# W2 and Wo of three chunks in four lanes of 32 rows around the next chunk's scores: a layer of window attention and gated MLP on one core

## The chip, the cores and the metric

The kernel runs on one NeuronCore of a Trainium2 chip. The time is the device time of one execution in microseconds. Its inputs and its output lie in the chip's memory, in bfloat16; sums are kept in float32 in PSUM, which has 8 banks of 512 columns. Names of engines: TensorE (PE; PEld is its weight load), VectorE (DVE), ScalarE (ACT), GpSimd (POOL) and SyncE (SP), which issues most of the DMAs.

## What is computed

For x of 2048 rows by 576, with 32 heads of 18 numbers, a window of 256 keys, and a hidden width of 4608:

```python
def _A_ref(x, wqkv, wo):
    B, S, D = x.shape
    H = 32; Dh = D // H; W = 256
    qkv = (lambda x, *d: x.transpose(*d))((x @ wqkv).reshape(B, S, 3, H, Dh), 2, 0, 3, 1, 4)
    q, k, v = qkv[0], qkv[1], qkv[2]
    scores = jnp.einsum("bhqd,bhkd->bhqk", q, k) * (Dh ** -0.5)
    idx = jnp.arange(S)
    mask = (idx[:, None] - idx[None, :] >= 0) & (idx[:, None] - idx[None, :] < W)
    scores = jnp.where(mask[None, None], scores, -1e9)
    p = _softmax(scores, axis=-1)
    o = jnp.einsum("bhqk,bhkd->bhqd", p, v)
    return (lambda x, *d: x.transpose(*d))(o, 0, 2, 1, 3).reshape(B, S, D) @ wo

def _B_ref(x, w1, w3, w2):
    gate = jnp.einsum("bsd,df->bsf", x, w1)
    up = jnp.einsum("bsd,df->bsf", x, w3)
    h = _silu(gate) * up
    out = jnp.einsum("bsf,fd->bsd", h, w2)
    return out

xn = _layernorm(x, axis=-1)
return x + _A_ref(xn, A_wqkv, A_wo) + _B_ref(xn, B_w1, B_w3, B_w2)
```

## The kernel before

The rows are worked off in four chunks of 512. A chunk has three parts on TensorE, one after the other.

First Q, K and V (`proj_part`): pairs of matmuls, one on rows 0 to 63 of the array and one on rows 64 to 127, with 512 columns for Q and K and 288 for V. Q and K are evacuated to `stage`, and DMAs repack them into `qv` and `kv` (`span_main`, `span_last`), four heads to a group, eight groups.

Then 36 units (`unit_pairs`), each of 128 hidden columns: nine pairs of matmuls of 512 columns for gate and up. ACT takes a tanh of the gate (`unit_tanh`), DVE forms the hidden value from it in two instructions (`unit_h`) and writes it to `hT`. Three pairs of PSUM banks rotate through the units. Between the pairs stand the steps of the scores: `scores` writes for one group, four heads at once, the scores of several blocks of 64 keys, 512 columns in two banks; `exps` is one exponential of 1024 columns on ACT; `masks` multiplies the diagonal blocks with a mask on POOL. A group has 5 steps (4 in chunk 0). When two groups are done, `pv` multiplies them with V, in tiles of 64 rows by 20 columns, eight of them side by side: the first pass after unit `FIRST`, the next two joined at `JOINT`, the last one after the units. Its result is turned, divided and packed into `oT` by DVE, POOL and DMAs.

Last W2 and Wo (`p2_item`): `hT` is the stationary operand, in blocks of 128 by 128, and W2 streams through it with 288 columns per matmul, 288 matmuls; `oT` with Wo is added to the same four banks, 32 matmuls on 128 rows and twice four on 64 rows (`wo_rest`). DVE adds x and SP stores the rows.

The order is written by the program: `add` puts each operation on the list of its engine, `resolve` derives the semaphore waits, and each engine works its list off in order. `later` puts work of DVE, POOL and SP behind a given unit; `spaced_step` spreads the score steps; `owe_part` hands out W13 loads (weights of gate and up, three buffers of four units each), `load_w2` the pieces of W2 (four buffers). Finished scores lie in slots (`pt` and buffers that are free at the time).

## Time and profile before

| | |
|---|---|
| median of 3 runs | 557.67 us (557.61 to 558.14) |
| span of the profiled execution (first to last instruction) | 555.9 us |
| one chunk's Q, K, V and units in that span (155.0 to 239.3) | 84.3 us |
| one chunk's W2 and Wo in that span (239.3 to 279.0) | 39.7 us |
| HBM read, written | 71.29 MB, 2.36 MB |
| DMA packets | 127217 |

The profile's page gives the span only, not the profiled execution's time with what lies around the span; the runs' median is 1.8 us above the span. Busy times on the page are sums per engine. Matmuls are pipelined, so a matmul's own length is longer than the distance from its start to the next one's. In the timeline a row is a group of like instructions: start, length from the first start to the last end, engine, line, operation, out<-in, shapes, count.

### The profile page before, as it was taken

The page shows a single profiled execution, that of the slowest core. Times are in us where ns is not written, and L with a number is a line of the kernel's source. Part 1 is how long each engine was busy: PE and PEld are TensorE (multiplying, and loading weights), DVE is VectorE, ACT ScalarE, POOL GpSimd, SP SyncE. Part 2 cuts the span into 40 slices and gives each one's busy share as a digit, 9 for nine tenths or more (in the row PEclk, how much of TensorE's full clock was granted, in tenths as well). Part 3 has the DMA queues.
Part 4 walks back from the last instruction along what each step waited for, and adds up shares of the span by engine and source line. Part 5 has one row for each costly group of instructions (what it writes and reads, how often), then busy time and mean ns, then how long its engine had stood idle before and what let it go on. Part 6 is the DMA issues. An engine that isn't in the chain of part 4 may idle for free.

```text
span 555.9 us, 15754 instructions
## 1 busy us (share of the span) xinstructions
PE 552.1 (99%) x6772; PEld 346.6 (62%) x6772; DVE 311.4 (56%) x583; ACT 260.0 (47%) x359; POOL 162.7 (29%) x385
## 2 busy tenths in 40 slices
PE   8999999999999999999999999999999999999998
PEld 4666554677665545477766544847776554455776
DVE  6566978610365888851056687874105577678211
ACT  6457766100387774700048787550005777756000
POOL 5424534300034452530003454333001334333000
PEclk9999999999999999999999999999999999999999
DMA  9995989577377469756826748485582674553552
GB/s 244 201 206 139 211 188 243 106 196 186 90 143 164 114 138 167 217 136 174 203 57 140 169 126 198 123 205 136 151 187 54 138 174 122 150 151 82 142 150 65
DMA packets 127217, 85.96 MB, mean 155 GB/s; under 512 B 34452, under 2 KB 124908, under 8 KB 127148
## 3 DMA queue, kind: packets, MB, share of 16 engines
q1 hardware_dynamic: 125523, 83.49, 64.1%
q10 hardware_dynamic: 1624, 1.47, 1.0%
q8 instruction: 53, 0.87, 0.7%
q14 instruction: 17, 0.13, 0.1%
HBM read 71.29 MB, written 2.36 MB: 133 GB/s over the span
## 4 chain that ended last, share of the span: by engine, by line
PE 99%; ACT 0%; DVE 0%; issue 0%
PE ps L713 50%; PE ps L785 25%; PE ps L461 10%; PE ps L587 6%; PE ps L644 3%; PE ps L792 3%; PE ps L827 1%; PE ps L699 0%; PE ps L406 0%; ACT xnT L413 0%; DVE ofin L803 0%; DVE oq L821 0%
## 5 line engine op out<-in xcount | busy, mean ns | idle before, releaser
L713 PE MATMUL ps<-xnT,w 64*128 64x512 bf16 x1400 | 185.4, 376 | 0.0
L713 PE MATMUL ps<-xnS,w 64*128 64x512 bf16 x1120 | 154.0, 376 | 0.0
L785 PE MATMUL ps<-w,hT 128*128 128x288 bf16 x1156 | 146.7, 286 | 0.0
L728 DVE SCALAR_TENSOR_TENSOR gs<-th,ps 128x512 bf16<-128x512 bf16 x144 | 97.8, 679 | 76.6 <-ACT th L722 75.8
L785 PEld LDWEIGHTS ps<-w,hT 128*128 128x128 bf16 x1156 | 112.5, 98 | 28.9 <-issue 0.4
L713 PEld LDWEIGHTS ps<-xnT,w 64*128 64x128 bf16 x1400 | 73.0, 94 | 60.0 <-DVE ofin L653 0.2
L722 ACT ACTIVATE th<-ps 128x512 bf16<-128x512 f32 x144 | 85.6, 594 | 44.4 <-PE ps L713 42.0
L731 DVE SCALAR_TENSOR_TENSOR hT<-gs,ps 128x512 bf16<-128x512 bf16 x144 | 98.9, 687 | 4.9
L713 PEld LDWEIGHTS ps<-xnS,w 64*128 64x128 bf16 x1120 | 58.1, 94 | 46.7
L596 ACT ACTIVATE pt<-ps 128x1024 bf16<-128x1024 f32 (+1 forms) x70 | 70.8, 1011 | 31.2 <-PE ps L587 30.9
L474 ACT ACTIVATE stage<-ps 128x512 bf16<-128x512 f32 x16 | 9.5, 596 | 142.0 <-PE ps L461 142.0
L803 DVE TENSOR_TENSOR ofin<-ps,xp 128x288 bf16<-128x288 f32 x31 | 13.4, 455 | 108.3 <-PE ps L699 58.1
L623 POOL TENSOR_TENSOR hT<-hT,mk 128x128 int32<-128x128 int32 (+1 forms) x59 | 24.0, 429 | 170.5 <-ACT hT L596 170.3
L623 POOL TENSOR_TENSOR pt<-pt,mk 128x128 int32<-128x128 int32 (+1 forms) x124 | 49.9, 427 | 28.8 <-ACT pt L596 28.8
L587 PE MATMUL ps<-qv,kv 64*128 64x320 bf16 (+4 forms) x528 | 52.8, 260 | 0.0
L587 PEld LDWEIGHTS ps<-qv,kv 64*128 64x128 bf16 x528 | 27.4, 94 | 26.2 <-ACT hT L596 1.5
L596 ACT ACTIVATE w<-ps 128x1024 bf16<-128x1024 f32 (+1 forms) x32 | 32.3, 1010 | 12.3 <-PE ps L587 12.2
L461 PE MATMUL ps<-xnT,wp 64*128 64x512 bf16 (+1 forms) x360 | 38.0, 355 | 0.0
L596 ACT ACTIVATE hT<-ps 128x1024 bf16<-128x1024 f32 (+1 forms) x32 | 32.3, 1010 | 5.3 <-PE ps L587 4.8
L623 POOL TENSOR_TENSOR w<-w,mk 128x128 int32<-128x128 int32 (+1 forms) x56 | 22.9, 429 | 28.8 <-ACT w L596 28.8
L666 DVE STREAM_TRANSPOSE od<-oq 128x256 bf16<-128x256 bf16 x64 | 25.8, 427 | 6.9 <-POOL oq L659 6.9
L461 PEld LDWEIGHTS ps<-xnT,wp 64*128 64x128 bf16 x360 | 19.0, 94 | 14.4 <-ACT stage L474 0.2
(93 smaller groups left out, 384.9 us busy)
## 6 DMA issues: line engine op xcount, KB each, us to landing
w<-in_B_w_dram SPq DMA_DIRECT2D x210, 192.0 KB, 3.9
w<-in_B_w_dram SPq DMA_DIRECT2D x72, 288.0 KB, 3.3
xp<-in_A_x_dram SPq DMA_DIRECT2D x30, 144.0 KB, 4.5
out_dram<-ofin SPq DMA_DIRECT2D x31, 72.0 KB, 1.7
xnS<-xnT SPq DMA_DIRECT2D x8, 256.0 KB, 4.2
oT<-od SPq DMA_DIRECT2D x40, 36.0 KB
pt<-in_A_wqkv_dram SPq DMA_DIRECT2D x4, 288.0 KB, 6.0
hT<-in_B_w_dram SPq DMA_DIRECT2D x6, 192.0 KB, 5.2
```

Of the source, the lines that this page charges most:

```text
L461: op = add("pe", lambda e, out_=out_, st=st, mv=mv, n=n, r0=r0, first=first: e.matmul(out_, st, mv, start=first, stop=(part == 1 and n == ...
L587: add("pe", lambda e, r0=r0, out_=out_, kb=kb, q0=q0, nb=nb: e.matmul(out_, kb4[r0:r0 + 64, g, kb + NV - NB, :] if kb < 0 else kv[r0:r0 + ...
L596: add("act", lambda e: e.activation(pt_slot(sl)[:, 0:w, :], PS[:, SC[0]:SC[1] + 1, 0:w].rearrange("p r q -> p q r"), ACT.Exp, scale=scale) ...
L623: add("pool", lambda e, vb=vb, mm=mm: e.tensor_tensor(vb, vb, mm, ALU.mult), r=(key if n == 0 else []) + ["mk"], **{"w" if n == 0 else "j" ...
L644: add("pe", lambda e, p=p, q=q, pr=pr, sl=sl, g=g, pos=pos, q0=q0, nb=nb, col=col, first=first, n=n: e.matmul(PS[32 * q:32 * q + VW, banks ...
L666: add("dve", lambda e: e.transpose(od[i][:, g % 2, c0:c0 + CH // 2], oq[:, c0:c0 + CH // 2]), r=["oq", "oq0"], **{"j" if half or g % 2 els ...
L713: op = add("pe", lambda e, n=n, r0=r0, r=r, k=k, src=src: e.matmul(PS[:, b0 + r, :], wt[r0:r0 + 64, k, fl * 128:(fl + 1) * 128], src, star ...
L722: add("act", lambda e: e.activation(th[i][:], PS[:, bg, :], ACT.Tanh, scale=0.5), r=[("ps", bg)], w=[("th", i)])
L728: add("dve", lambda e: e.scalar_tensor_tensor(out=gs[i][:], in0=th[i][:], scalar=1.0, in1=PS[:, bg, :], op0=ALU.add, op1=ALU.mult), r=[("t ...
L731: add("dve", lambda e: e.scalar_tensor_tensor(out=hT[:, u, :], in0=gs[i][:], scalar=0.5, in1=PS[:, bu, :], op0=ALU.mult, op1=ALU.mult), r= ...
L785: add("pe", lambda e: e.matmul(bank, hT[:, f, tt * 128:(tt + 1) * 128], w2[sl][:, k, n0:n1], start=first, stop=(c + 1 == NC and half == 1 ...
L792: add("pe", lambda e: e.matmul(bank, oT[:, k, tt * 128:(tt + 1) * 128], wo[:, k, d0 + n0:d0 + n1], start=False, stop=(k == 3 and (half == ...
```

## The change

For the W2 part of chunks 0, 1 and 2, the array is used as four lanes of 32 rows and 128 columns (`w2_lanes`). W2 is now stationary and `hT` streams, 512 columns per matmul: lane a holds rows 32a to 32a+31 of every 128 hidden columns and sums into its own bank; for each of four blocks of 128 output columns it has 36 matmuls of W2 and 4 or 5 of Wo. At the end of a block `finish` adds the four banks (two copies on ACT, three additions on DVE), and a DMA turns the result. Four banks are summed into while the four others take scores. The last 64 output columns follow as 41 pairs of matmuls of 256 columns, side by side in two tiles of 64 output columns.

Q, K and V of the next chunk move ahead of this part, from behind it. Sixteen of the next chunk's heads (groups 0 to 3) get their scores in the lanes, between the matmuls of W2: one head per lane, 18 rows, blocks of 128 keys, three steps of 512 columns per head (`score_new`), an exponential of 512 columns (`exps_new`), and a mask that DVE applies (`masks_new`). Their P V (`pv_new`) runs on all 128 rows in tiles of 20 columns, four side by side, in two passes: one after two groups, within the lanes, the other after the last 64 columns of W2. Groups 4 to 7 stay between the units in the old form, and their two P V are joined (`JOINTS`). The chunk's result is added to x and stored in units 4 to 7 of the next chunk. Chunk 3 has its W2 and Wo as before. W2 is loaded in pieces of 9 blocks by 128 columns (and 18 by 64), W13 in two halves per block from its third block on, where six parts were.

```diff
@@ load_w2 @@
+        def w2_by(s, nd):
+            return w2[s][:, :, :].rearrange("p f d -> p (f d)").rearrange("p (f d) -> p f d", d=nd)
+
...
+            if n2fill <= (NC - 1) * 2 * NFC:
+                if m < 16:
+                    dst, f0, nf, d0, nd = w2_by(s, 128), m % 4 * 9, 9, m // 4 * 128, 128
+                else:
+                    dst, f0, nf, d0, nd = w2_by(s, 64), (m - 16) * 18, 18, 512, 64
+                add("sp", lambda e: e.dma_start(
+                    dst, B_w2[f0 * 128:(f0 + nf) * 128, d0:d0 + nd].rearrange("(fl p) d -> p fl d", p=128)),
+                    w=[("w2", s)], after=after, dma=f"w2_{s}")
+                return
...
+        STEPS = [[(-2, 0, 1), (0, 0, 3)], [(-1, 0, 2), (2, 2, 2)], [(1, 1, 3), (3, 3, 1)]]
+        EDGES = [[(0, 2, 0), (3, 1, 0)], [(1, 2, 0)], [(2, 2, 0), (0, 1, 1)]]
...
+        def score_new(g, s, a, b, n):
+            jb, q0, nb = STEPS[s][n]
+            c0 = 128 * n * STEPS[s][0][2]
+            add("pe", lambda e: e.matmul(
+                PS[:, b, c0:c0 + nb * 128], kn[32 * a:32 * a + Dh, g, W + 128 * jb:W + 128 * jb + 128],
+                qv[32 * a:32 * a + Dh, g, q0 * 128:(q0 + nb) * 128], start=True, stop=True, tile_position=(32 * a, 0)),
+                r=[("knp" if jb < 0 else "kn", g), ("q", g)], **{"j" if n else "w": [("ps", b)]})
+
+        def exps_new(g, s, a, b, sl):
+            p = a % 2
+            add("act", lambda e: e.activation(head_of(sl, p), PS[:, b, :], ACT.Exp, scale=scale),
+                r=[("ps", b)], **{"j" if p else "w": pt_keys(sl)})
+
...
+                mm = mkn[:, k0:k0 + nb, :].unsqueeze(1).to_broadcast([128, 2, nb, 64])
+                add("dve", lambda e, b0=b0, nb=nb, mm=mm: e.tensor_tensor(
+                    v[:, :, b0:b0 + nb, :], v[:, :, b0:b0 + nb, :], mm, ALU.bitwise_and),
+                    r=(key if n == 0 else []) + ["mkn"], **{"w" if n == 0 else "j": key})
...
+                    for p in range(2):
+                        for q in range(4):
+                            g, pr = 2 * j + q // 2, q % 2
...
+                            add("pe", lambda e, p=p, q=q, pr=pr, sl=sl, g=g, blk=blk, q0=q0, nb=nb, col=col, first=first, n=n: e.matmul(
+                                PS[32 * q:32 * q + VW, banks[p], q0 * 128:(q0 + nb) * 128],
+                                van[:, blk, 4 * g + 2 * pr + p, :],
+                                head_of(sl, p)[:, col * 128:(col + nb) * 128],
+                                start=first, stop=(n == n_all), tile_position=(0, 32 * q), skip_group_check=True),
+                                r=pt_keys(sl) + [("vn", blk)], **{"w" if new else "j": [("ps", banks[p])]})
...
+        def w2_lanes(c, live, pool_):
+            n = c + 1
+            for a in range(4):
+                for d_ in range(4):
+                    own = [("w2", d_, f) for f in range(NF)] + [("wo", d_, t) for t in range(4)]
+                    if (a < 2) == (d_ % 2 == 0):
+                        own.append(("wo", d_, 4))
+                    items[a] += [it + (k == 0, k == len(own) - 1) for k, it in enumerate(own)]
...
+            def finish(d_):
+                ls = sets[d_ % 2]
+                add("act", lambda e: e.activation(psum2, PS[:, ls[0], :], ACT.Copy), r=[("ps", ls[0])], w=[("th", 0), ("th", 1)])
+                add("act", lambda e: e.activation(psum3, PS[:, ls[2], :], ACT.Copy), r=[("ps", ls[2])], w=["psum3"])
+                for k in (1, 3):
+                    add("dve", lambda e, k=k: e.tensor_tensor(psum2, PS[:, ls[k], :], psum2, ALU.add),
+                        r=[("ps", ls[k])], w=[("th", 0), ("th", 1)])
+                add("dve", lambda e: e.tensor_tensor(gs[i][:], psum3, psum2, ALU.add),
+                    r=["psum3", ("th", 0), ("th", 1)], w=[("gs", i)])
+                events.setdefault(rounds + SEND_AFTER, []).append(("turn", d_))
...
+                if done < len(steps) and steps[done][2] * 2 + steps[done][3] == a and now >= nxt and (slots or steps[done][3]):
+                    cand = [b for b in sets[1 - d_ % 2] if b not in held]
+                    b = min(cand, key=lambda x: ready[x])
+                    if ready[b] <= now and left_in(items, at, a, clk) > 1.25:
...
+                        score_new(g, s, a, b, 0)
...
+                    add("pe", lambda e, b=b, rows=rows, wt=wt, fl=fl, k=k, a=a, first=first: e.matmul(
+                        PS[:, b, :], wt[rows, fl, :], hT[rows, k, :], start=first, stop=False, tile_position=(32 * a, 0)),
+                        r=[("h", k), ("w2", sl)], **{"w" if first else "j": [("ps", b)]})
...
+                    add("pe", lambda e, b=b, rows=rows, k=k, a=a, d_=d_, last=last: e.matmul(
+                        PS[:, b, :], wo[rows, k, d_ * 128:(d_ + 1) * 128], oT[rows, k, :], start=False, stop=last, tile_position=(32 * a, 0)),
...
+                if not pv_done and 0 in ended and not any(tail) and min(at) > 2 * 41 + 5 and now > ended[0] + PV_WAIT:
...
+                    pv_new(n, 0, cand)
...
+                        add("pe", lambda e, k=k, r=r, sl=sl: e.matmul(
+                            PS[64 * r:64 * r + 64, b, 0:256], w2_by(sl, 64)[:, k % 18, :], hT[:, k, 256 * r:256 * r + 256],
+                            start=(k == 0), stop=False, tile_position=(0, 64 * r), skip_group_check=True),
...
+                        add("pe", lambda e, t=t, r=r, wt=wt: e.matmul(
+                            PS[64 * r:64 * r + 64, b, 0:256], wt, oT[:, t, 256 * r:256 * r + 256],
+                            start=False, stop=(t == 4), tile_position=(0, 64 * r), skip_group_check=True),
...
+            banks = job()
+            pv_new(n, 1, banks)
+            add("dve", lambda e: e.tensor_copy(orem, PS[:, b, 0:256]), r=[("ps", b)], w=["orem"])
+            add("sp", lambda e: e.dma_start_transpose(frem, orem), r=["orem"], w=["frem"], dma="tr4")
...
+        def fin_add(tt):
+            x = xp[fin_xs[tt]]
+            r, j = divmod(tt, 2)
+            add("dve", lambda e: e.tensor_tensor(fin[:, tt, 0:512], fin[:, tt, 0:512], x[:, 0:512], ALU.add),
+                r=[("xp", fin_xs[tt])], w=[("fin", tt)])
...
-        FIRST = {0: 14, 1: 11, 2: 8, 3: 11}
-        JOINT = {0: (27, 6), 1: (27, 5), 2: (24, 8), 3: (27, 8)}
-        AHEAD = [40, 24, 40, 24]
+        FIRST = 15
+        JOINTS = [(27, 6), (31, 6), (32, 5), (25, 7)]
+        AHEAD, ALL_DONE = 40, [0, 276, 284, 215]
+        W2_FIRST, W2_SPACE, PV_WAIT = 2.2, 0.53, 3.0
+        W2_REPACK, SEND_AFTER = 40, 15
+        W2_EVENTS = {148: (("part",),), 156: (("part",),)}
...
-                        spaced_step()
+                fin_xs[:] = load_four(c - 1)
+                pv_out(late_pv[0], 0)
+                pv_out(late_pv[1], 1)
+                o_scale(0)
...
+            if c + 1 < NC:
+                if c == 0:
+                    banks = job()
...
+                for m, what in enumerate(PROJ_LATER + [None]):
+                    got = proj_begin(c + 1, what) if what else proj_end()
+                    if m == 0:
...
+                    if got == ("q", 2):
+                        new_k(0)
+                        new_k(1)
...
+                    if 3 <= m < 7:
+                        new_q(m - 3, "act")
+                    owe_part(last_pe())
+                i_last = (job_ctr - 1) % 3
+                live = [*SC, *JOBS[(i_last + 1) % 3]]
+                late_pv = w2_lanes(c, live, [*JOBS[(i_last - 1) % 3], *JOBS[i_last]])
+                continue```

How this moves the instructions. On PE, before, from the last P V of chunk 0 into W2 (`w2_0` to `w2_3` are the four buffers of W2; L644 is P V, L785 W2, L792 Wo):

```order
L644 MATMUL ps<-pt,va 20x320 x8
L644 MATMUL ps<-pt,va 20x128 x8
L785 MATMUL ps<-w2_0,hT 128x288 x16
L785 MATMUL ps<-w2_1,hT 128x288 x16
L785 MATMUL ps<-w2_2,hT 128x288 x16
L785 MATMUL ps<-w2_3,hT 128x288 x16
```

And in the changed kernel, from the end of the next chunk's Q, K, V (L496) into the lanes (L1036 is W2 in lanes, L756 a part of a score step):

```order
L496 MATMUL ps<-xnT,wp 128x256 x8
L496 MATMUL ps<-wv,xnT 128x288 x8
L1036 MATMUL ps<-hT,w2_0 128x512 x36
L1036 MATMUL ps<-hT,w2_1 128x512 x8
L756 MATMUL ps<-qv,kn 128x128
L1036 MATMUL ps<-hT,w2_1 128x512 x3
L756 MATMUL ps<-qv,kn 128x384
L1036 MATMUL ps<-hT,w2_1 128x512 x4
L756 MATMUL ps<-qv,kn 128x128
L1036 MATMUL ps<-hT,w2_1 128x512 x3
L756 MATMUL ps<-qv,kn 128x384
L1036 MATMUL ps<-hT,w2_1 128x512 x8
```

A score step is a matmul of 128 and one of 384 columns (or 256 and 256) in the same lane; two steps come to 18 matmuls of W2, and a W2 buffer now serves 36 of them.

On PE, before, at the end of W2 of chunk 0 and into the next chunk's Q, K, V (L461; L699 is the rest of Wo on 64 rows):

```order
L785 MATMUL ps<-w2_1,hT 128x288 x4
L792 MATMUL ps<-wo,oT 128x288 x4
L699 MATMUL ps<-wo,oT 128x288 x4
L461 MATMUL ps<-xnT,wp 128x512 x28
L461 MATMUL ps<-wv,xnT 128x288 x10
```

And in the changed kernel (L1045 is Wo in lanes, L1086 and L1096 the last 64 columns, and L791 the first of the 48 matmuls of the new P V, behind which the next chunk's units begin):

```order
L1036 MATMUL ps<-hT,w2_3 128x512 x36
L1045 MATMUL ps<-oT,wo 128x512 x18
L1086 MATMUL ps<-hT,w2_0 64x256 x36
L1086 MATMUL ps<-hT,w2_1 64x256 x36
L1096 MATMUL ps<-oT,wo 64x256 x8
L1096 MATMUL ps<-oT,wz 64x256 x2
L791 MATMUL ps<-stage,va 20x128 x2
L791 MATMUL ps<-pt,va 20x128 x2
```

W2 now ends in the tail of 64 columns and a P V, and the Q, K, V that stood here are gone.

On ACT, which had no instruction during W2 of chunk 0, the changed kernel has this in the lanes (L763 are exponentials of scores, L987 and L988 the copies of `finish`):

```order
L547 ACTIVATE va<-ps 64x8x18 x2
L763 ACTIVATE pt<-ps 128x512 x11
L987 ACTIVATE thb<-ps 128x512
L988 ACTIVATE kv<-ps 128x512
L763 ACTIVATE pt<-ps 128x512 x9
L763 ACTIVATE xp<-ps 128x512 x4
L763 ACTIVATE stage<-ps 128x512
L987 ACTIVATE thb<-ps 128x512
L988 ACTIVATE kv<-ps 128x512
```

The copies that empty the lanes' banks stand behind the exponentials of the scores before them.

496 lines of the change are left out of this document (374 added, 122 removed).

## Prediction

> **What bounds the kernel now.** I read the page first, then the chain, then the timeline of TensorE stage by stage.
>
> ```profile
> span 555.9 us, 15754 instructions
> PE 552.1 (99%) x6772; PEld 346.6 (62%) x6772; DVE 311.4 (56%) x583; ACT 260.0 (47%) x359; POOL 162.7 (29%) x385
> PE ps L713 50%; PE ps L785 25%; PE ps L461 10%; PE ps L587 6%; PE ps L644 3%; PE ps L792 3%; PE ps L827 1%; PE ps L699 0%; PE ps L406 0%; ACT xnT L413 0%; DVE ofin L803 0%; DVE oq L821 0%
> ```
>
> TensorE is the whole chain, and nothing else has a visible share of it: gate and up L713, W2 L785, Q K V L461, scores L587, P V L644, Wo L792. A busy PE need not be PE at its peak, so I measure the pace by starts in the timeline of chunk 1 (start us, us, what):
>
> ```profile
> 92.44 8.63 PE ps L713 x80
> ...
> 237.68 0.41 PE L699 MATMUL ps<-wo,oT 64*128 64x288 bf16 x4
> 238.03 0.32 PE L644 MATMUL ps<-stage,va 64*20 64x320 bf16 x4
> ...
> 239.34 16.34 PE L785 MATMUL ps<-w,hT 128*128 128x288 bf16 x132
> 255.52 0.65 PE L792 MATMUL ps<-wo,oT 128*128 128x288 bf16 x4
> ...
> 278.06 0.65 PE L792 MATMUL ps<-wo,oT 128*128 128x288 bf16 x4
> 278.64 0.42 PE L699 MATMUL ps<-wo,oT 64*128 64x288 bf16 x4
> 278.90 1.46 PE L461 MATMUL ps<-xnT,wp 64*128 64x512 bf16 x12
> ```
>
> The first row is from the chain: 40 pairs of 64-row matmuls in 8.63 us, 0.216 us a pair of 512 columns. A W2 matmul of 288 columns takes (255.52 - 239.34)/132 = 0.1226 us. The two paces give 0.417 ns a column and some 0.0025 us per instruction, and the stretches join without holes: the kernel is a list of columns on one engine. So the change pays only through fewer columns, less cost per instruction, or fewer changes between tile shapes; any wait it brings is paid in full.
>
> **The change, part by part (chunks 1 to 3 for scores and P V, 0 to 2 for W2).**
>
> Scores. The rows of one score step between units:
>
> ```profile
> 174.88 0.32 PE L587 MATMUL ps<-qv,kv 64*128 64x320 bf16 x2
> 175.02 0.27 PE L587 MATMUL ps<-qv,kb 64*128 64x128 bf16 x4
> 175.10 1.26 PE L713 MATMUL ps<-xnT,w 64*128 64x512 bf16 x10
> ```
>
> A step takes 175.10 - 174.88 = 0.22 us; a chunk has 8 groups of 4 heads with 5 steps, 8.8 us. Afterwards four groups keep this form, 20 x 0.22 = 4.4 us. The other 16 heads take 3 steps each, 48 steps that each stream 512 columns through one of four lanes: 48 x 0.216/4 = 2.6 us. That is 8.8 - 7.0 = 1.8 us a chunk, **-5.4 us** in three. It is the main gain: four lanes write 512 scores per column where two write 256, and a block of 128 keys needs 384 queries instead of 320 for 64.
>
> W2 and Wo. Before: 0.35 us for the four L699 ahead of P V, and 278.90 - 239.34 = 39.56 us, together 39.9 us. After: a lane holds 4 x (36 + 4) matmuls and 2 of the rest of Wo, 162 rounds. The trace has no four lanes, so I bound a round: 0.216 us is what two lanes of 512 columns take, and no row streams 512 columns faster; if only two of the four ran at once it would be 0.432. I take 0.216, because the nearest rows on concurrency are the L644 matmuls above, eight tiles that share one stream: 96 of them between 238.03 and 239.34. So 162 x 0.216 = 35.0 us. The last 64 columns of W2 are 41 pairs of 256 columns; the nearest rows are the pairs of 256 of L461:
>
> ```profile
> 291.57 0.62 PE L461 MATMUL ps<-xnT,wp 64*128 64x256 bf16 x8
> 292.01 0.67 PE L461 MATMUL ps<-wv,xnT 64*128 64x288 bf16 x8
> ```
>
> 0.44/4 = 0.11 us a pair, 4.5 us. Sum 39.5 us, -0.4 us a chunk, **-1.2 us**.
>
> P V. One pass alone takes 239.34 - 238.03 = 1.31 us. Two joined:
>
> ```profile
> 217.05 1.37 PE L644 MATMUL ps<-pt,va 64*20 64x320 bf16 x96
> ...
> 219.50 0.82 PE L713 MATMUL ps<-xnS,w 64*128 64x512 bf16 x6
> ```
>
> 2.45 us, so a second one costs 1.14 and a trip into this shape and out again 0.17. A chunk had 2.45 + 2 x 1.31 = 5.07 us. The new form streams 12 blocks x 128 x 2 = 3072 columns per tile where the old one has 2560: 1.14 x 3072/2560 = 1.37, with the trip 1.54 (bounds 1.37 and 1.54). Chunk after: 2.45 + 2 x 1.54 = 5.53, +0.46, **+1.4 us** in three.
>
> Changes of shape. The four L792 from 278.06 take 4 x 0.1226 = 0.49 us at pace, but L699 starts after 0.58: 0.09 us a change. Q K V to lanes and lanes to the last 64 columns are two more per chunk (bounds 0 and 0.17 each), **+0.5 us**. Q, K and V have the same matmuls, only earlier; chunk 3's W2 stays as it was.
>
> Sum: -5.4 - 1.2 + 1.4 + 0.5 = **-4.7 us**.
>
> **What must stay hidden.** Q, K, V ahead fill the 13 us between the last unit and W2, and W2 in lanes now hides 48 exponentials and 8 copies that were not there. In that stretch before:
>
> ```profile
> 239.30:279.00 39.70, 39.70 (x334) 31.54 (x328) 6.60 (x17) 0.00 (x0) 4.69 (x11) 1.00 0.69 174
> L722 ACT ACTIVATE th<-ps 128x512 bf16<-128x512 f32 x144 | 85.6, 594 | 44.4 <-PE ps L713 42.0 <-DVE hT L731 1.5
> 60.61 0.60 ACT L722 ACTIVATE th<-ps 128x512 bf16<-128x512 f32 x1 [0.38 <-PE ps L713]
> 61.10 0.91 ACT L596 ACTIVATE pt<-ps 128x896 bf16<-128x896 f32 x1
> L731 DVE SCALAR_TENSOR_TENSOR hT<-gs,ps 128x512 bf16<-128x512 bf16 x144 | 98.9, 687 | 4.9
> ```
>
> (columns: PE, PEld, DVE, ACT, POOL busy, clock, DMA share, GB/s). ACT had 0.00 us there, DVE 6.60, and the granted clock was 1.00. A 512-wide ACT instruction lasts 0.594 us, but the next can start 0.49 us after it (60.61 to 61.10). In the order of the lanes two score steps come per 18 W2 matmuls: 4.5 rounds x 0.216 + 2 x 0.054 = 1.08 us, one exponential per 0.54 us. That lies between the two ends, nearer to the pace of 0.49, which I take: 56 x 0.49 = 27.4 us in some 39. Scores use the four PSUM banks of the next 128 columns, each again after four steps, 2.2 us. DVE gets 40 masks, no wider than half an L731, and 12 additions as wide, at most 40 x 0.4 + 12 x 0.69 = 24 us (the 0.4 is my estimate from half of 0.687), and the masks are needed only by P V, 3 us and more later.
>
> The result of a chunk is now added and stored in units 4 to 7 of the next one, on DVE, which has room in that stage:
>
> ```profile
> 155.00:239.30 84.30, 84.30 (x1231) 45.38 (x1226) 63.78 (x116) 59.24 (x77) 34.85 (x83) 1.00 0.72 158
> ```
>
> 63.78 of 84.30 us. The 64-key masks of half the heads leave POOL there, and half the exponentials leave ACT. If DVE fell behind, units would wait for PSUM, but eight additions of at most 0.69 us spread over four units can't make up the 20 us that are free.
>
> The queues. W2 pieces of 288 KB now have 256 B to a packet instead of 576:
>
> ```profile
> q1 hardware_dynamic: 125523, 83.49, 64.1%
> w<-in_B_w_dram SPq DMA_DIRECT2D x72, 288.0 KB, 3.3
> ```
>
> A packet holds an engine 0.641 x 16 x 555.9/125523 = 45 ns for 665 B on average. A piece was 32 packets per engine, 1.5 of its 3.3 us; it becomes 72, between 72 x 45 x 256/665 = 1.3 us (by bytes) and 3.3 us (by count), so it lands 3.1 to 5.1 us after its issue. It is issued when its buffer's old piece is used up and needed three pieces later, 27 rounds = 5.8 us: hidden at both ends. SP's other work that moves into the lanes (repacking of groups 4 to 7, five transposes, two W13 halves) waits for engines that are ahead; a late transpose would hold W2 loads queued behind it. The four Q moves are on ACT's queue between evacuations of Q K V, where no exponential waits any more. The W13 weights of four units still come two such blocks ahead, 8 x 9 x 0.216 = 15.6 us, now in two halves instead of six parts.
>
> The Trainium skill (DMA: Bandwidth & Descriptors, Specifications) asks for at least 512 B to a transfer and says that below this there is a read-modify-write. It speaks against 256 B pieces: at half the rate per byte a piece would take 3.0 us instead of 1.5 and land after about 4.8, an estimate, which is still inside the lead. The mixed packets above cannot decide it.
>
> **Rivals.**
>
> *A, the lanes do not overlap: slower.* Each further lane starts behind the one before it. Two 320-column matmuls cover 0.32 us (row at 174.88), and one lasts 0.297:
>
> ```profile
> L587 PE MATMUL ps<-qv,kv 64*128 64x320 bf16 x256 | 39.8, 297 | 0.0
> ```
>
> so a lane starts 0.02 us after the other. If two more lanes lengthen each round by that, it is 0.26 us, 486 rounds x 0.044 = +21 us, **574 us**; with two at a time, +105 us. It decides from 4.7/486 = 10 ns a round on. Against it: eight tiles of L644 share a stream without this. For it: those write 20 columns each, and no row has more than two tiles of 128. The Trainium skill (TensorE: Matmul & The Clock Gate, Part 3, measured speedup) gives 3.07x for four row tiles of 32 instead of 4; as a lasting pace that would be an estimate of 0.216 x 4/3.07 = 0.281 us a round, +32 us, 585 us. No run here shows it.
>
> *B, ACT falls behind.* If an exponential costs 0.594 us and not 0.49, a burst of 14 ends 14 x 0.054 = 0.76 us late, the copies that empty the banks come behind it, and TensorE waits 0.3 to 0.7 us at each of 12 block changes: +3.6 to +8.4 us, **556.6 to 561.4**, no change or slightly slower. For it: the exponential waits for TensorE each time. Against: 0.49 in the rows.
>
> *C, a moved transfer is late* (a W2 piece behind a transpose on SP, or Q and K of the new heads at the first score): 0.5 to 1 us at some 10 places, **558 to 563**.
>
> **How the numbers follow.** The page's span is 555.9 us; the runs' median, 557.67, lies 1.8 us above it, which I take as the part around the span, unchanged. Forecast 557.7 - 4.7 = **553.0 us**. Its own range: without the trips and changes of shape 551.5, and 0.0025 us less per round if instructions cost nothing in the lanes, 550; with a few small waits 555.5. Chances: forecast 0.72, A 0.11, B 0.11, C 0.06. A change below 0.2% (1.1 us) can't be told from none. Range 550 to 558.5: it leaves out A, most of C and the far half of B. Faster (under 556.5): 0.72 and a third of B and C, 0.78. Same: 0.06. Slower: 0.16.
>
> **What would show it.** Lanes: 36 matmuls of W2 ahead of the first score in 9 x 0.216 = 1.9 us and the stage in about 39 us (A: over 45). PE without idle time in the lanes, ACT some 30 us busy there (B: PE idle behind ACT copies at the block changes). A score step in units still 0.22 us, 20 per chunk. W2 pieces landing under 5.8 us (C). I am wrong if a round of four is over 0.226 us, or if TensorE stops for PSUM banks.

## Result: 554.2 us where 557.7 was, and the profile after

The changed kernel took a median of **554.22 us** (552.73 to 556.97, six runs) beside 557.75 us (557.61 to 558.14, six runs) for the kernel before: a ratio of 0.9939, 95% interval 0.9921 to 0.9956. The same kernel once more (e1) took 553.51 us (553.23 to 554.77, five runs) beside 557.69, ratio 0.9927, interval 0.9913 to 0.9940. So it is 0.6 to 0.7% faster, 3.5 and 4.2 us. The forecast was 553.0 us in a range of 550.0 to 558.5. The profiled run took 553.22 us with a span of 551.5.

From the page of the changed kernel, the lines that answer to those of before: the span, the engines, the chain, and two DMA queues (packets, MB, share).

```profile
span 551.5 us, 17660 instructions
PE 547.4 (99%) x7690; PEld 302.4 (55%) x7690; DVE 364.5 (66%) x745; ACT 294.5 (53%) x481; POOL 120.5 (22%) x281
PE ps L860 51%; PE ps L1036 17%; PE ps L496 10%; PE ps L932 6%; PE ps L682 4%; PE ps L1086 2%; PE ps L1045 2%; PE ps L739 2%; PE ps L791 2%; PE ps L756 1%; DMA wv<-in_A_wqkv_dram 1%; PE ps L939 1%; PE ps L1096 0%; SPq L311 0%; ACT xnT L447 0%; PE ps L846 0%
q1 hardware_dynamic: 164622, 85.42, 79.1%
q8 instruction: 60, 0.98, 0.8%
```

The chain is still TensorE, now with the lanes (L1036, L1045, L756) in it, and it has a new first link: 1% of it is the load of V's weights. ACT and DVE do 35 and 53 us more than before, POOL 42 us less. DMA engines are busy for 79% in place of 64%. By the DMA records, packets of 128 to 576 bytes make a quarter of this rise (W2 comes in 256 bytes now, the last two pieces of a chunk in 128). Two thirds are in packets of 1024 bytes, nearly all W13's: about as many as before, but 84 ns each in place of 67. The queue of instruction fetches, 60 packets of 16 KB, was no part of the prediction; it comes up below.

The three stretches of lanes, by windows of the changed kernel (busy us and count of PE, PEld, DVE, ACT and POOL; granted clock, DMA share, GB/s); a stretch lasts 39.3 us with the new P V in it, of which the windows leave out the last 1.4:

```profile
115.90:153.80 37.90, 37.90 (x774) 21.10 (x776) 22.66 (x60) 30.14 (x57) 1.35 (x2) 1.00 0.71 139
251.30:289.20 37.90, 37.90 (x774) 21.26 (x776) 22.62 (x60) 30.14 (x57) 1.35 (x2) 1.00 0.70 137
386.80:424.70 37.90, 37.90 (x774) 21.39 (x776) 22.67 (x60) 30.14 (x57) 1.35 (x2) 1.00 0.75 147
```

All three are alike: no hole on PE, clock 1.00, ACT busy for 30.14 of 37.90 us, DVE for 22.7. The timeline of PE at the start and the end of the first stretch:

```profile
115.86 2.55 PE L1036 MATMUL ps<-hT,w 32*128 32x512 bf16 x44
118.24 0.22 PE L756 MATMUL ps<-qv,kn 18*128 18x128 bf16 x1
...
155.12 4.12 PE L1086 MATMUL ps<-hT,w 128*64 128x256 bf16 x72
...
159.72 0.23 PE L791 MATMUL ps<-stage,va 128*20 128x128 bf16 x2
...
161.14 1.04 PE L860 MATMUL ps<-xnT,w 64*128 64x512 bf16 x8
```

The first score comes after 44 matmuls, as in the order shown under the change; the prediction had counted 36 and 1.9 us. They take 118.24 - 115.86 = 2.38 us, 0.0541 each or **0.216 us a round of four**. The new P V takes 161.14 - 159.72 = 1.42 us. In the same stretch, grouped by line and shape (busy us and mean ns; then the idle time ahead and its releaser):

```profile
L763 ACT ACTIVATE pt<-ps 128x512 bf16<-128x512 f32 x40 | 21.7, 594 | 2.6 <-PE ps L756 2.5
L771 DVE TENSOR_TENSOR pt<-pt,kv 128x256 int32<-128x256 int32 x20 | 8.3, 422 | 8.3 <-ACT pt L763 8.1
```

ACT waits for TensorE's scores (2.5 us), not the other way round. From the start of each group of TensorE to the start of the next, summed by kind of work over the whole execution (us, worked out from the starts in the two traces):

```
                                   before    after
units (L713, L860)                 280.38   280.43
scores between units (L587, L682)   33.37    19.74
W2 and Wo, 128 rows (L785, L932 ..) 159.96    40.19
lanes, their scores included            -   113.54
last 64 columns (L1086, L1096)          -    13.79
P V, old form (L644, L739)          19.09    11.29
P V, new form (L791)                    -     8.53
Q, K, V (L461, L496)                52.86    53.83
before and between these             6.59     6.56
sum                                552.25   547.90
```

### The profile page after: what moved, and what is told of

Read it like the earlier page. It is cut to its first block, busy times and chain, and to the rows that moved or that the text cites. A ratio compares the mean times of both kernels' runs of the same rounds, so it can differ in the third digit from the quotient of the medians.

```text
span 551.5 us, 17660 instructions
## 1 busy us (share of the span) xinstructions
PE 547.4 (99%) x7690; PEld 302.4 (55%) x7690; DVE 364.5 (66%) x745; ACT 294.5 (53%) x481; POOL 120.5 (22%) x281
## 3 DMA queue, kind: packets, MB, share of 16 engines
q1 hardware_dynamic: 164622, 85.42, 79.1%
## 4 chain that ended last, share of the span: by engine, by line
PE 98%; DMA 1%; SPq 0%; ACT 0%; issue 0%; DVE 0%
PE ps L860 51%; PE ps L1036 17%; PE ps L496 10%; PE ps L932 6%; PE ps L682 4%; PE ps L1086 2%; PE ps L1045 2%; PE ps L739 2%; PE ps L791 2%; PE ps L756 1%; DMA wv<-in_A_wqkv_dram 1%; PE ps L939 1%; PE ps L1096 0%; SPq L311 0%; ACT xnT L447 0%; PE ps L846 0%
## 5 line engine op out<-in xcount | busy, mean ns | idle before, releaser
L860 PE MATMUL ps<-xnT,w 64*128 64x512 bf16 x1400 | 177.0, 376 | 0.0
L860 PE MATMUL ps<-xnS,w 64*128 64x512 bf16 x1120 | 147.8, 376 | 0.0
L875 DVE SCALAR_TENSOR_TENSOR gs<-thb,ps 128x512 bf16<-128x512 bf16 x144 | 97.8, 679 | 60.6 <-ACT thb L869 60.0
L869 ACT ACTIVATE thb<-ps 128x512 bf16<-128x512 f32 x144 | 85.6, 595 | 77.1 <-PE ps L860 76.2
L1036 PE MATMUL ps<-hT,w 32*128 32x512 bf16 x1728 | 106.9, 374 | 0.0
L860 PEld LDWEIGHTS ps<-xnT,w 64*128 64x128 bf16 x1400 | 67.2, 94 | 70.2
L860 PEld LDWEIGHTS ps<-xnS,w 64*128 64x128 bf16 x1120 | 53.9, 94 | 58.1
L1036 PEld LDWEIGHTS ps<-hT,w 32*128 32x128 bf16 x1728 | 57.6, 92 | 29.6 <-issue 1.4
L763 ACT ACTIVATE pt<-ps 128x512 bf16<-128x512 f32 x120 | 65.1, 594 | 7.7 <-PE ps L756 7.5
L756 PE MATMUL ps<-qv,kn 18*128 18x384 bf16 (+2 forms) x288 | 54.5, 267 | 0.0
L771 DVE TENSOR_TENSOR pt<-pt,kv 128x256 int32<-128x256 int32 x96 | 31.3, 371 | 24.5 <-ACT pt L763 24.1
L496 PE MATMUL ps<-xnT,wp 64*128 64x512 bf16 (+1 forms) x360 | 38.2, 355 | 0.1
L932 PE MATMUL ps<-w,hT 128*128 128x288 bf16 (+1 forms) x292 | 36.9, 284 | 0.0
L756 PEld LDWEIGHTS ps<-qv,kn 18*128 18x128 bf16 x288 | 26.5, 93 | 14.4 <-DVE uq L800 0.8
L932 PEld LDWEIGHTS ps<-w,hT 128*128 128x128 bf16 x292 | 28.2, 98 | 7.4 <-issue 0.5
L682 PE MATMUL ps<-qv,kv 64*128 64x320 bf16 (+4 forms) x336 | 31.7, 258 | 0.0
```

What stands on the lines that cost most here:

```text
L496: op = add("pe", lambda e, out_=out_, st=st, mv=mv, n=n, r0=r0, first=first: e.matmul(out_, st, mv, start=first, stop=(part == 1 and n == ...
L682: add("pe", lambda e, r0=r0, out_=out_, kb=kb, q0=q0, nb=nb: e.matmul(out_, kb4[r0:r0 + 64, g - GN, kb + NV - NB, :] if kb < 0 else kv[r0: ...
L756: add("pe", lambda e: e.matmul(PS[:, b, c0:c0 + nb * 128], kn[32 * a:32 * a + Dh, g, W + 128 * jb:W + 128 * jb + 128], qv[32 * a:32 * a + ...
L763: add("act", lambda e: e.activation(head_of(sl, p), PS[:, b, :], ACT.Exp, scale=scale), r=[("ps", b)], **{"j" if p else "w": pt_keys(sl)})
L860: op = add("pe", lambda e, n=n, r0=r0, r=r, k=k, src=src: e.matmul(PS[:, b0 + r, :], wt[r0:r0 + 64, k, fl * 128:(fl + 1) * 128], src, star ...
L869: add("act", lambda e: e.activation(th[i][:], PS[:, bg, :], ACT.Tanh, scale=0.5), r=[("ps", bg)], w=[("th", i)])
```

## The experiments

Each starts from the changed kernel. "Lanes" is the time from the first lane matmul to the last 64 columns, without the P V among them, a chunk: 37.85 us in the changed kernel. Where an edit adds lines, the numbers behind it shift: L1038 and L1039 are L1036 of the changed kernel, L1088 is L1086, L861 and L863 are L860.

### e1: once more

No edit.

> The changed kernel once more, nothing edited, to see whether its runs scatter again and where. Seen so far: 552.7 to 557.0 us (median 554.22), the kernel before 557.6 to 558.1. Theory (the list of columns on TensorE is as forecast, and what scatters is a wait for a weight transfer, at the start or at the lanes): the stages of the new trace agree with the first one within 0.1 us each, apart from the first 22 us or the start of the lanes; median 552.7 to 554.5. Rival (ACT or DVE falls behind in the lanes in some runs, B): the lanes L1036+L756+L1045 take more than 38.2 us a chunk in a slow profile, where the first trace has 37.85.

553.51 us, lanes 37.85 us again, units 280.43. What differed from the first trace was Q, K, V at the start (0.2 us) and the joined P V of chunk 0, 2.30 us in place of 1.92. Its weight loads, in the timeline of e1:

```profile
83.15 0.08 PEld L739 LDWEIGHTS ps<-w,va 64*20 64x20 bf16 x1 [0.30 <-issue]
```

TensorE stopped in the middle of a P V with nothing to wait for that the profile shows. So ACT does not make this scatter, and waits for weights make no more than the 0.2 us at the start; what "issue" stands for had to be found.

### e2 and e3: the price of a score in the lanes

```diff
+            for k in range(2):      # e2: each score matmul twice
                 add("pe", lambda e: e.matmul(PS[:, b, c0:c0 + nb * 128], kn...
```
```diff
-                PS[:, b, c0:c0 + nb * 128], kn...          # e3: an eighth of the columns
+                PS[:, b, c0:c0 + nb * 16], kn...
-            ... e.activation(head_of(sl, p), PS[:, b, :], ACT.Exp, scale=scale)
+            ... e.activation(head_of(sl, p), PS[:, b, :], ACT.Copy)
```

> Every score matmul of the 16 heads in the lanes is issued twice in a row into the same PSUM columns. Theory (a step costs its 512 columns in one of four lanes, 0.054 us, and nothing waits): 144 x 0.054 = +7.8 us against the changed kernel, the lanes 40.4 us a chunk. A second matmul in the same lane right behind the first waits for it, so if neighbours in the queue must be of different lanes to overlap, it costs up to 0.216 us more than its share: 144 x 0.16 = +23 us. Rival B (the stage is set by ACT): less than +4 us, since TensorE would only fill time in which it waits.

> Every score matmul in the lanes streams an eighth of its columns, and the 48 exponentials of a chunk are copies of the same shape (the scores of these 16 heads are not computed, ACT has the same work). Theory (columns): 7/8 of 7.8 us goes, -6.8 us against the changed kernel, lanes 35.6 us a chunk. If a score matmul costs a fixed time beside its columns (its weights, its place in the queue): -3 to -5 us. Rival B (ACT sets the pace): within 1.5 us of the changed kernel.

e2: 564.84 us (564.15 to 567.87), lanes 40.78 us, so 2.93 us a chunk or 0.061 us a step. That is the priced 0.054 and a little, and not the 0.216 that a second matmul of the same lane would add if it held the others up. e3: 547.94 us (547.81 to 548.28), 5.6 us less than e1; lanes 36.07 us, 1.78 us less. Seven eighths of the columns were priced at 2.26 us a chunk; about 0.5 us, 10 ns a step, stays with the step and not with its columns. Rival B (ACT sets the pace) is out here: TensorE's time followed its own work both ways.

Of e2's profiled span, 14.6 us longer, only 8.8 are lanes. 3.2 us are in old P V and 2.4 in units. The timeline of PE in e2, in the middle of the joined P V of chunk 2 and behind it, and the windows around it (columns as above, the clock third from the end):

```profile
375.47 0.23 PE L739 MATMUL ps<-pt,va 64*20 64x128 bf16 x2 [1.87 <-issue]
...
376.56 2.06 PE L861 MATMUL ps<-xnT,w 64*128 64x512 bf16 x10
```
```profile
376.50:380.50 4.00, 4.00 (x26) 1.49 (x22) 3.03 (x7) 0.60 (x1) 0.58 (x1) 0.57 0.02 4
380.50:384.20 3.70, 3.70 (x38) 1.66 (x36) 2.71 (x5) 1.20 (x2) 0.10 (x1) 1.00 0.58 128
```

A stop of 1.87 us, again put down to issue, and behind it four microseconds at a granted clock of 0.57, in which ten matmuls took 2.06 us (1.26 in the row at 175.10 of before). This stop is paid nearly twice; one of 2.03 us in e10, below, is not.

### e4, e8 and e11: how the lanes share the queue

```diff
+                if stick is not None:
+                    a = stick
...
                 at[a] += 1
+                stick = a if at[a] % N else None     # N = 2 (e4), 9 (e8), 4 (e11); e8 and e11 up to item 150 of a lane
```

> In the lanes each lane now issues two W2 or Wo matmuls in a row before the next lane's turn (0 0 1 1 2 2 3 3 in place of 0 1 2 3), with the same work in all. Rival A as a question of order: if TensorE starts its instructions in the order of the queue and a lane must end one matmul before its next, eight matmuls take 4 x 0.216 us instead of 2 x 0.216, so 486 rounds take 0.432 us: about +100 us (650 us). If a later instruction of a free lane may overtake, or two of one lane overlap otherwise: within 5 us of the changed kernel.

> Each lane now issues up to nine W2 or Wo matmuls in a row before the next lane's turn (e4: two in a row, no loss), with the score steps planned 0.45 us apart in place of 0.53. Theory (a lane's matmuls wait in a queue of their own while those of another lane, later in the order, start; the depth is unknown): if the look ahead is deep enough for 27 matmuls, within 2 us of the changed kernel; if it is a few matmuls, the lanes follow one another for most of nine: up to 486 x 0.216 x 0.8 = +80 us (635 us).

> Each lane issues four W2 or Wo matmuls in a row before the next lane's turn (two: no loss, 554.0 us; nine: 906.6 us), with the score steps planned 0.50 us apart. Theory (TensorE starts a matmul while a bounded number of earlier ones in other lanes still wait): if the bound is 12 or more, within 2 us of the changed kernel; if it is 4 to 8, lanes follow one another for part of each round of sixteen: a pace between 0.216 and 0.8 us a round, +20 to +250 us, and a granted clock well under 1 in the lanes as with nine.

One run each: two in a row 554.0 us (lanes 38.2 us a chunk), four 593.04 (50.6), nine 906.6 (154.2). The first 5 us of lanes in the changed kernel, by windows, and then in e4, e11 and e8, with a later stretch of e8 (PE's count is the first in brackets):

```profile
116.00:121.00 5.00, 5.00 (x102) 2.67 (x98) 1.53 (x6) 3.15 (x8) 0.00 (x0) 1.00 0.21 47
```
```profile
116.00:121.00 5.00, 5.00 (x106) 3.79 (x97) 1.23 (x5) 2.87 (x8) 0.00 (x0) 1.00 0.25 54
```
```profile
116.00:121.00 5.00, 5.00 (x78) 2.82 (x75) 1.60 (x4) 2.25 (x6) 0.00 (x0) 1.00 0.19 44
```
```profile
116.00:121.00 5.00, 5.00 (x42) 2.29 (x39) 1.19 (x3) 0.86 (x3) 0.00 (x0) 1.00 0.19 43
160.00:195.00 35.00, 35.00 (x145) 13.66 (x143) 2.90 (x9) 7.16 (x12) 0.00 (x0) 0.50 0.17 34
```

In 5 us 102, 106, 78 and 42 matmuls are under way, all at clock 1.00. With two of one lane in a row next to nothing is lost (0.3 us a chunk), so a lane that is busy does not hold up the next lane's matmul; with four a quarter is lost, and with nine the lanes mostly follow one another. In e8 it gets worse: from 126 us on the clock is 0.50, although PE counts as busy throughout, and in the stretch shown 145 matmuls take 35 us, 0.241 us each against 0.054. They have 65,536 columns, 128 times 512; at half the clock 512 columns take 0.43 us, so on average 1.6 lanes are at work. The look-ahead between lanes is real and short. How many instructions it holds was not measured; e8 and e11 also have their scores 0.45 and 0.50 us apart instead of 0.53. The values of the result also change in e8 and e11; why stays open, so that more than the order may differ there.

### e6: more work for ACT

```diff
                     exps_new(g, s, a, b, sl)
+                    if p and pr:
+                        exps_new(g, s, a, b, sl, True)
```

> In the lanes 12 of the 48 exponentials of a chunk are done twice, into the same place, so ACT has 12 x 0.594 = 7.1 us more to do in a stage of 37.85 us of which it was busy for 30.1. Theory by the sum of the stage (it still fits, and the scores' PSUM banks are four deep): within 1 us of the changed kernel. Theory by the pace (rival B just over its edge): five exponentials take 5 x 0.49 = 2.45 us where four steps come in 4 x 0.53 = 2.12, twelve times over, so ACT ends a good 4 us behind, of which the gaps between bursts and the free banks take some 1 to 2: TensorE waits 2 to 3 us a chunk, +6 to +9 us, and the waits stand at score matmuls for ACT's exponentials.

563.77 us (562.87 to 564.59), 10.3 us over e1; lanes 40.95 us, +3.1 a chunk, 9.3 in three. From what PE waited for in e6 (us in all, times, longest), and its timeline there:

```profile
PE ps L1038 <- ACT stage L763: 3.6, 3, 1.2
```
```profile
138.94 0.40 PE L1038 MATMUL ps<-hT,w 32*128 32x512 bf16 x3 [1.20 <-ACT stage L763]
```

TensorE stops at a change of 128 columns for a PSUM bank whose exponential is not done: the place that rival B names. Such stops of PE are 3.6 of the 9.3 us; the rest is waits of its weight loads and shorter gaps. 7.1 us more on ACT would still fit into the 7.8 us that it has free in a stretch; it does not fit the pace of the bursts. So the margin is under 12 exponentials a chunk.

### e7: W2 pieces asked for later

```diff
-                        if piece[m] == 4:
+                        if piece[m] == 4 and m:
                             load_w2((c + 1) * 2 * NFC)
+                        if piece[m] == 4 and m == 15:
+                            load_w2((c + 1) * 2 * NFC)
```

> In the lanes each W2 piece is asked for one piece later (nine rounds, about 2 us, less lead: when its buffer's old piece and the one after it are used up), so the lead falls from 27 rounds (5.8 us, some 6.5 with the scores between) to 18 (3.9 to 4.4 us). Rival C's margin: pieces landed a median 3.9 us after their issue, some later. Theory (the transfer was hidden by about 2 us): about half of the 12 pieces of a chunk are now late by up to 1 us, +1 to +4 us a chunk, +3 to +12 us. If the true lead is larger than I count, since TensorE's weights are read late or SP issues early: within 0.5 us of the changed kernel.

566.57 us (565.81 to 571.18), +13.1 us. But the lanes took 38.2 us: the loss is in the last 64 columns, 24.2 us in place of 11.9 for L1086, over the three chunks. What PE waited for in e7:

```profile
PE ps L1088 <- DMA w<-in_B_w_dram: 8.5, 4, 2.9
PE ps L1036 <- DMA w<-in_B_w_dram: 0.2, 1, 0.2
```

The 16 pieces of 128 columns still come in time with 2 us less lead, but for some 1 us in chunk 2, half of it a wait for the first of the last two. The last piece does not. The timeline of PE in e7 where it is needed in chunk 0, and SP's at the end of the lanes of chunk 1, first in the changed kernel and then in e7, where this stretch begins 3.9 us later (L379 issues W2 pieces, L343 W13):

```profile
159.29 3.29 PE L1088 MATMUL ps<-hT,w 128*64 128x256 bf16 x36 [2.33 <-DMA w<-in_B_w_dram]
```
```profile
287.44 0.58 SPq L379 DMA_DIRECT2D w<-in_B_w_dram  x1
288.07 1.99 SPq L343 DMA_DIRECT2D w<-in_B_w_dram  x2
```
```profile
290.29 0.59 SPq L379 DMA_DIRECT2D w<-in_B_w_dram  x1
290.92 1.33 SPq L343 DMA_DIRECT2D w<-in_B_w_dram  x1
292.30 0.62 SPq L379 DMA_DIRECT2D w<-in_B_w_dram  x1
```

Measured from the start of the stretch, the last piece is asked for only 1.0 us later (0.7 and 2.1 in chunks 0 and 2), but a W13 load of 576 KB now goes out ahead of it. It landed 7.2 and 7.4 us after its issue in chunks 0 and 2 (chunk 1 has no record), against 4.0 to 4.2 in the changed kernel. That the W13 load causes this is likely and was not tested alone. TensorE waits 2.3 to 2.9 us for it in each chunk, and the clock is 0.50 for 3.4 us behind each wait. My count of leads was right for the lanes and missed where the tight place is: the last piece. In the changed kernel that one, issued at 287.44, landed 4.0 us later and was needed at about 292.6 (18 pairs, 2.0 us, after 290.57): a margin of 1 us.

### e5 and e9: the joined P V elsewhere

```diff
-        JOINTS = [(27, 6), (31, 6), (32, 5), (25, 7)]
+        JOINTS = [(27, 6), (34, 6), (35, 5), (25, 7)]      # e5 and e9
-                if joint[0] < u:
+                if (27, 31, 32, 25)[c] < u:                # e9 only
```

> The joined P V of chunks 1 and 2 move later by 27 pairs of unit matmuls (JOINTS 31,6 to 34,6 and 32,5 to 35,5); all work is the same. Counted in TensorE's own instructions (a weight load and a matmul each, and its waits), they began at 250 and 252 of a block of 256 and ended without a stop (2.46 and 2.47 us); they now begin near 102 and 104. In e2 a joined P V that began at 124 stopped for 2.0 us in its middle with nothing to wait for but its next instructions, and the units after it ran 1.8 us longer. Theory (a stop for the next block of instructions, which a P V uses up faster than it is fetched, is what the joint's place avoids, and such stops make the scatter of the runs): +2 to +4 us for each of the two, +4 to +8 us in all, and a profile that shows P V at 4 us or more with an idle time put down to issue. Rival (the stop in e2 was a chance collision with other DMA traffic, and the place within a block does not matter): within 0.5 us of the changed kernel.

> As e5 (the joined P V of chunks 1 and 2 begin 27 pairs of unit matmuls later, near 102 and 104 of a block of 256 instructions), but W2 pieces for the lanes are asked for in the same units as in the changed kernel; in e5 they had moved behind the joint, and the lanes of chunk 2 waited 25.6 us for them. Theory (instruction blocks): each of the two stops in its middle for 2 to 4.5 us with nothing to wait for but its instructions (e5: 6.93 and 5.21 us in place of 2.46), and what follows runs up to 2.5 us longer at a lower granted clock, so +6 to +14 us against the changed kernel, with lanes of 37.9 us a chunk. Rival (e5's stops came from the moved loads): P V at 2.5 us and within 1 us of the changed kernel.

e5: 602.21 us (601.74 to 603.84). Two joined P V took 6.93 and 5.21 us, but most of the 49 us is the side effect that the second text names: W2 for the lanes of chunk 2 was asked for behind the joint. What PE waited for in e5:

```profile
PE ps L1036 <- DMA w<-in_B_w_dram: 25.6, 8, 4.2
PE ps L739 <- issue: 7.0, 3, 4.1
```

e9: 567.12 us (565.77 to 567.94), lanes 37.85 us again, the two P V 6.78 and 9.52 us. Here W2 pieces land in buffers that hold probabilities the later P V still reads, so P V waits for them and its values change. In e9's list of waits, and the timeline of PE in the first P V:

```profile
PE ps L739 <- DMA w<-in_B_w_dram: 6.7, 2, 4.8
PE ps L739 <- issue: 2.0, 1, 2.0
```
```profile
239.87 0.20 PE L739 MATMUL ps<-od,va 64*20 64x64 bf16 x3 [2.04 <-issue]
...
240.67 2.26 PE L860 MATMUL ps<-xnT,w 64*128 64x512 bf16 x10
```

So 6.7 of e9's 13.6 us are waits for these loads, and the instruction stop of 2.04 us stands at the same matmul of P V as in e5 (behind 173 weight loads), with the slow units after it. In chunk 2, where P V had already waited 4.8 us, it has no stop at that point: probably the wait gave the fetch its time. So the theory's range of +6 to +14 us is met only with waits that were not in its sum, and of its two stops one came.

I numbered TensorE's instructions in the order of the trace (a weight load and a matmul each, and semaphore waits). Ten stops for issue inside a P V, in seven profiles (e1, e2, e5, e6, e8, e9, e10), all stand at number **193 or 194 of a block of 256** (the text ahead of e12 says twelve profiles; seven have such a stop). Stops of PE for issue among the units stand there too, to within three (up to 1.3 us in e2, e3, e5 and e12). The trace has 60 fetches of 16 KB for some 15,500 instructions, 258 to a fetch. So these are edges of instruction blocks. P V uses up a block in 1.6 us, the lanes in 6.5, the units in 12 to 13. For chunk 0's joined P V, with one edge behind its 79th weight load, the DMA records give how long after the edge before it the fetch began, and the time between the two edges (us):

```
            fetch begins   edge to edge
before          1.37           6.00
changed         2.82           6.02
e11             2.92           6.03
e9              2.93           6.02
e7              3.08           6.15
e3              3.22           6.16
e4              3.24           6.02
e1              3.65           6.41
e8              3.66           6.50
e2              4.04           7.01
e5              4.10           6.96
e6              4.40           7.27
```

Up to some 3.2 us the P V runs through (e3 and e7 lose 0.1 us); beyond it the second number is the first plus 2.8 to 3.0. A block can be used about 2.9 us after its fetch begins to move, and each block is fetched about when the one before it is begun. The Trainium skill (Advanced Engine Details and Errata, ISA Cache) gives lines of 16 KB, 256 instructions; these traces agree with that size, and the stops 256 apart show it.

### e10: chunk 0's joint ten pairs earlier

```diff
-        JOINTS = [(27, 6), (31, 6), (32, 5), (25, 7)]
+        JOINTS = [(26, 5), (31, 6), (32, 5), (25, 7)]
```

> The joined P V of chunk 0 begins ten pairs earlier (JOINTS 27,6 to 26,5), near 239 of its block of 256 instructions in place of 35; the other three are as in the changed kernel (231 to 252, 2.45 to 2.48 us in each of its profiles). At 35 it took 1.92, 2.30, 2.05, 1.92, 2.04 us in the profiles of the changed kernel, e1, e3, e4 and e7, and 2.85 to 3.17 in e5 and e6. Theory (this stop makes most of the scatter and of what the median lies above the forecast): 1.90 to 1.95 us in the profile, median 552.3 to 553.3 us where the changed kernel had 554.22 and 553.51, and a spread of at most 1 us. Rival (the scatter comes from the start or from elsewhere): median and spread as in e1.

555.69 us (554.63 to 557.49): slower than e1, the theory's place was wrong. P V took 4.65 us; its timeline in e10:

```profile
83.70 0.20 PE L739 MATMUL ps<-hT,va 64*20 64x64 bf16 x3 [2.03 <-issue]
```

I had taken the number in the block at which the other joints begin as the rule, before I knew where the edge lies. Ten pairs earlier more of P V comes ahead of the edge, and without the stop the time from edge to edge falls from 6.02 to 6.78 - 2.03 = 4.75 us. The fetch began 4.00 us after the first edge, and 6.78 = 4.00 + 2.78 fits the table. What counts is the time between two edges, not the place of the start. The clock did not fall behind this stop, as it did in e2, e5 and e9; the window behind it in e10:

```profile
84.30:88.30 4.00, 4.00 (x51) 1.99 (x48) 3.35 (x7) 3.03 (x4) 0.87 (x2) 1.00 1.68 170
```

By that count of time between edges the edge would best fall in the middle of P V; this was not tried.

### e12: smaller transfers in chunk 0

```diff
-                dst[64 * n:64 * n + 64, a:b, :], ...
+            for x in range(a, b, 3):                # blocks 2 to 8 of chunk 0
+                dst[64 * n:64 * n + 64, x:min(x + 3, b), :], ...
```

> The W13 weights of chunk 0 (blocks 2 to 8) are asked for at the same places, but each transfer of 576 KB (or 320 and 256 KB) as pieces of at most 192 KB one right behind the other, the size that the kernel before used; nothing else is edited. Counted in TensorE's instructions, every stop in a P V that was put down to issue came at the same point of a block of 256 (193 or 194, twelve profiles). In the kernel before the fetch of 16 KB after the edge ahead of chunk 0's joined P V began 0.86 to 1.37 us behind that edge, in the changed kernel and its variants 2.8 to 4.4 us, and the block can be used some 2.8 us after its fetch begins: with 3.2 us and less there is no stop in the 6.02 us between the two edges, with 4.4 us one of 1.3 us. Theory (a fetch waits behind a large transfer that is under way): fetches begin 0.5 to 2 us after the edge as before, P V takes 1.90 to 1.95 us, the runs lie within 1 us of one another and the median is 552.5 to 553.4 us. Rival (what delays the fetch is how much is to be moved at that time, not in what pieces): fetches begin 2.8 us or more after the edge, median and scatter as in e1 (553.5 us, 1.5 us).

557.16 us (555.09 to 560.85, 11 runs), ratio 0.998 to the kernel before: most of the gain is gone. For this P V the fetch began 2.26 us after its edge, sooner than in any run of the changed kernel in the table, and the P V had no stop for issue (0.9 of its 2.96 us were a wait for a hidden value). But at three other edges of chunk 0 it took 3.5 to 4.4 us, so not all of them came back to the 0.9 to 2.3 us of before. That speaks against the size of the transfers as the cause; it is no clean test, since SP's whole queue moved. SP's timeline in e12, and what PE waited for:

```profile
59.17 9.68 SPq L346 DMA_DIRECT2D w<-in_B_w_dram  x14
```
```profile
PE ps L1039 <- DMA w<-in_B_w_dram: 2.0, 1, 2.0
PE ps L863 <- issue: 1.3, 1, 1.3
```

Fourteen issues hold SP for 9.68 us, 0.69 each whatever their size; keys and W2 pieces behind them come late. The 1.3 us for issue stand among the units, at number 196. The split costs 3.6 us here, so fewer issues are probably worth something by themselves.

## Why the prediction was right, and where its sizes were off

**The bound.** A list of columns on TensorE, where each wait is paid in full: right. The sums by kind of work give -4.35 us, the forecast was -4.7, and the whole of it is in the kinds that the change touches, the units the same to 0.05 us. Part of this is luck: P V came out 0.7 us cheaper than forecast and Q, K, V 1.0 us dearer, and the two nearly cancel. By the runs' medians the gain is 3.5 and 4.2 us.

**Scores, W2 and changes of shape.** These three terms were -5.4, -1.2 and +0.5, together -6.1. Measured: scores between units -13.63, W2 and Wo with their scores 113.54 + 13.79 + 40.19 - 159.96 = +7.56, together **-6.07**. A lane stretch was forecast at 35.0 + 2.6 = 37.6 us and took 37.85. A second score step cost 0.061 us in e2, and e3 saved 0.037 us for seven eighths of its columns, 0.042 for all of them; the rest is a cost per step. The agreement is in part luck: the scores between units fell by 0.4 us more than forecast (13.2), and lanes and last columns took 0.5 us more.

**Rival A** is out. A round took 0.216 us, the pace of 2 lanes with 4, where A needed 0.26. The Trainium skill (TensorE: Matmul & The Clock Gate, Part 3) gives 3.07x for four row tiles of 32; by that the stretch would have been about 162 x 0.281 + 2.6 = 48 us, an estimate, and the trace has 37.85. The same section says that matmuls start and end strictly in order; with two of a lane in a row that would have cost e4 about 100 us, and it cost 1 us in three chunks. e8 and e11 show what is left of the rival: overlap needs the lanes to take turns within a few instructions.

**P V** was mis-sized: 1.54 was taken, from bounds of 1.37 and 1.54, and it is 1.42 each. The term is +0.73 us instead of +1.4 (11.29 + 8.53 - 19.09). The step that failed is the choice of the upper end of the bounds. Its 3072 columns at 0.417 ns are 1.28 us, and 0.14 is all that comes on top, where the forecast had 0.26. A likely reason is that the 1.14 us for a second P V already held a cost per matmul (the new P V has 48, the old one 96), which I scaled by columns before I added the trip of 0.17; no run tests this.

**What must stay hidden.** ACT was forecast at 27.4 us in the lanes and "some 30 us busy"; it is busy for 30.14. DVE 22.7 us, forecast at most 24. The W2 pieces issued in the lanes land 3.0 to 5.0 us after their issue (forecast 3.1 to 5.1); the rows of the changed kernel, and the landing of the 54 pieces in the new form (its longest, some 10 us, were asked for far ahead):

```profile
w<-in_B_w_dram SPq DMA_DIRECT2D x60, 576.0 KB, 6.9
w<-in_B_w_dram SPq DMA_DIRECT2D x72, 288.0 KB, 3.9
DMA to landing us min/median/max: 3.0/4.1/10.6
```

The 3.9 us hold the 18 pieces of chunk 3 as well, which are in the old form; the new ones took a median of 4.1. Before, a piece took 3.3 us with packets of 576 bytes. Smaller packets are dearer by 0.8 us, hidden as forecast. The Trainium skill (DMA: Bandwidth & Descriptors, Specifications) asks for at least 512 B to a transfer; the prediction's estimate of half the rate would have made it 1.5 us. The prediction gave all pieces 256 bytes to a packet; the last two of a chunk have 128, twice as many packets. Rivals B and C did not occur, but e6 and e7 show that they were near and where: B at the change of 128 columns, less than 12 exponentials away; C only at the last W2 piece, about 1 us away.

**What the prediction did not have.** First, the start: Q, K, V take 0.97 us more, of which about half at the start. What PE waited for in the changed kernel:

```profile
PE ps L1160 <- DVE oq L1154: 1.2, 1, 1.2
PE ps L496 <- DMA wv<-in_A_wqkv_dram: 0.2, 1, 0.2
```

The second row is new: TensorE meets V's weights 0.2 us before they are there. Which edit of the loads at the start does it was not tried. Second, instruction fetches. I read the fixed P V at 2.45 us and never asked what else a stream of short matmuls uses up. They explain most of where the profiles of this kernel and its variants differ in chunk 0's joined P V, by 0 to 1.3 us. That they also make the spread of the timed runs (552.7 to 557.0 us beside 0.5 to 1.2 us for the kernel before) is likely and not shown, since only profiled runs have a trace. Why the fetch begins later in chunk 0 than before (2.8 to 4.4 us against 1.37) stays open; e12 speaks against the size of the transfers. No experiment with the same work was faster than the changed kernel beyond its scatter.

## What to carry to other kernels

When TensorE has no holes, a change is a sum of columns divided by the lanes that share them, and such a sum held to 0.4 us in 550 here, in part because two errors cancelled. But the lanes must take turns in the queue: two in a row still overlapped, four did so only in part. Where a stretch of short matmuls uses up a block of 256 instructions faster than the next can arrive, its place against the edges of the blocks is part of its cost: look for idle time put down to issue, number the instructions, and leave as much time as possible from edge to edge. A margin is found by taking a little of it away: e6 and e7 say more about how safe this kernel is than any busy share.
